# Order and distance of the loads in a linear attention step: alpha, then k and q, then v, and v two chunks ahead

## The chip, the cores and the metric

The kernel runs on one core of a Trainium2 chip. Its time is the device time of one execution in microseconds; of several executions the median is given. A profile is one further execution, recorded by the hardware profiler.

The engines are named as the profile names them: PE is TensorE (PEld its weight loads), DVE is VectorE, ACT is ScalarE, POOL is GpSimd, SP is SyncE, which in this kernel only issues DMA transfers (its queue is SPq). L144 is line 144 of the kernel.

## The reference

Two blocks follow each other. The first is a gated linear attention over 4 batches and 8 heads, 768 positions, head size 48, computed position by position:

```
state = alpha[t][:, None] * state + outer(k[t], v[t])
y[t]  = q[t] @ state
```

The second takes y as 3072 tokens of 384 features (8 heads times 48) and computes

```
a = x @ w1;  b = x @ w2          # 384 -> 1024 each
out = ((a * b) @ w3) @ w_out     # 1024 -> 1024 -> 384
```

Everything is float32 in the reference; the second block's weights arrive as 64-bit floats.

## The kernel before

**Attention in chunks.** The positions are cut into chunks of 128: six per batch, N = 24 in all, handled for all heads at once. For chunk n, `logs(n)` takes the logarithm of alpha on ACT (L271), `decays(n)` sums it along the positions with a triangular matrix on PE (L286 or L289) and takes exponentials on ACT (L292, L293), `decayed(n)` multiplies q and k by them on DVE (L302), `transposed(n)` transposes q and k on PE (L324) and copies them to `qkT` on ACT (L326), `scores(n)` multiplies them within the chunk on PE (L364), masked on DVE into `ms` (L367). `outer(n)` forms the sums of k and v that carry the state to the next chunk (PE L336, then DVE L344 or L346); the last chunk of a batch has none. The output comes from `attend_state(n)` (PE L384, the state's part) and `attend(n)` (PE L390, the chunk's own scores times v). Its copy on ACT (L394) is queued for a store to the DRAM buffer `xd`, written by SP at the next step's beginning (`store`, L261).

The chunk v(n) is thus read first by `outer(n)`, in step n of the main loop, and last by `attend(n)`, in step n + 1.

**Loads.** `load_a` (L132), `load_kq` (L138 for k, L139 for q) and `load_v` (L144) each issue transfers of 192 KB on SP's queue. alpha and the pair of k and q rotate through three buffers each. v has five fixed tiles, `vs`, made once with AHEAD = 4 in `AHEAD + 1`; v(n) lies in tile n modulo 5. Before the main loop the loads of the first chunks are issued with the setup and the first chunk's work between them. In step n of the main loop SP's part is, in the order of the source: the stores of the chunk before, a load of x back from `xd` in five of the steps (L406), then v(n + 3), alpha(n + 5), and k and q of n + 4.

**Weights.** The 64-bit weights w1 and w2 come in blocks of 512 KB (`raw`, L192, on the same SP queue), are turned into float32 on ACT and DVE and split into parts (`to_fp32`, `load_gates`, L200 to L221), with a third part formed on PE (`third`, L232 and L233) and copied by ACT (L234). `convert` and `fetch` deal this out in portions over the steps; four `raw` buffers exist.

**The gates and the rest.** From step 6 on x of three chunks is split into three parts (`split_x`, L412 on ACT, L413 and L414 on DVE), and the products with w1 and w2 (L420) are laid into the steps from 7 on as pieces of fill (`run`). After the main loop come the remaining gates, the product of w3 and w_out (`fold`, L522), and the last products with their output (`project`), again with L420 as the matmul's line.

**What sets the order.** The source gives each engine's instructions an order, and `after_marks` pins some of them behind named ones. Otherwise the order of each engine's queue is made when the kernel is built, by going through the program with estimates of when each input will be there; an instruction can stand behind others that follow it in the source. On the chip an engine runs its queue in that fixed order, and SP's queue in the profile is that of the source.[...]

Of the kernel before, what the change touches and what calls it, by code (L numbers as in the profile page):

```python
# [48 lines left out]
def kernel(  # L49
# [27 lines left out]
    AHEAD = 4  # L77
# [30 lines left out]
    def after_marks(*names):  # L108
        stack = ExitStack()
        for x in names:  # L110
            stack.enter_context(tc.issue_after(mark[x]))
        return stack
# [12 lines left out]
    def rows(src, n):  # L125
        b, c = divmod(n, NCH)
        return src[b, :, ds(c * C, C), :].rearrange("h p d -> p h d")

    def load_a(n):
        if n < N:  # L130
            st["a", n] = inp.tile([C, H, D], FP32, tag="ac", name="ac")
            nc.sync.dma_start(out=st["a", n], in_=rows(alpha, n))  # L132

    def load_kq(n):
        if n >= N:
            return
        st["kq", n] = inp.tile([C, 2, H, D], FP32, tag="kq", name="kq")
        nc.sync.dma_start(out=st["kq", n][:, 0], in_=rows(k, n))  # L138
        nc.sync.dma_start(out=st["kq", n][:, 1], in_=rows(q, n))  # L139

    def load_v(n):
        if n < N:
            st["v", n] = vs[n % len(vs)]
            nc.sync.dma_start(out=st["v", n][:, :, 0:D], in_=rows(v, n))  # L144
# [91 lines left out]
    def fetch(ahead=3):  # L236
        while weights and len(begun) < ahead:
            begun.append(weights.popleft())
            next(begun[-1])
# [17 lines left out]
    def store():  # L257

        while later:
            dst, src = later.popleft()  # L260
            nc.sync.dma_start(out=dst, in_=src)  # L261
# [4 lines left out]
    def logs(n):  # L266
        if n >= N:
            return
        a = st.pop(("a", n)).rearrange("p h d -> p (h d)")
        la = st["la", n] = work.tile([C, DM], FP32, tag="la", name="la")  # L270
        nc.scalar.activation(la, a, AF.Ln)  # L271
        if n >= LATE:

            t = st["la", n] = work.tile([C, 2, DM], FP32R, tag="la2", name="la2", bufs=1)
            nc.scalar.copy(t[:, 0], la)
            nc.vector.tensor_sub(t[:, 1], la, t[:, 0].bitcast(FP32))
        if n in ends:
            nc.gpsimd.dma_start(out=ends[n][2:3], in_=a[0:1])

    def decays(n):  # L280
        if n >= N:
            return
        lc = bank()[:, 0:DM]
        la = st.pop(("la", n))
        if n < LATE:
            nc.tensor.matmul(lc, sums[:, n % 2].bitcast(FP32), la, start=True, stop=True)  # L286
        else:
            for i in range(2):
                nc.tensor.matmul(lc, sums[:, n % 2], la[:, i], start=(i == 0), stop=(i == 1))  # L289

        e = st["e", n] = work.tile([C, 2, DM], FP32, tag="e", name="e", bufs=3)
        nc.scalar.activation(e[:, 0], lc, AF.Exp, scale=-1.0)  # L292
        mark["e", n] = nc.scalar.activation(e[:, 1], lc, AF.Exp).ins  # L293
        if n in ends:
            nc.gpsimd.dma_start(out=ends[n][0:1], in_=e[0:1, 0])
        if n + 1 in ends:
            nc.gpsimd.dma_start(out=ends[n + 1][1:2], in_=e[C - 1:C, 1])
        load_ends(n)

    def decayed(n):  # L300
        if n < N:
            mark["qk", n] = nc.vector.tensor_mul(qks[n % 3][:, :, :, 0:D], st.pop(("kq", n)),  # L302
                                 st.pop(("e", n)).rearrange("p i (h d) -> p i h d", h=H)).ins
# [9 lines left out]
    def transposed(n):  # L313
        if n >= N:
            return
        qk = qks[n % 3]
        qkT = work.tile([C, 2, NP, C], FP32, tag="qkT", name="qkT")

        tp = [bank().rearrange("p (i j c) -> p i j c", i=2, j=NP) for _ in range(2)]
        for i in range(2):  # L320
            for j in range(NP):
                for half in range(2):
                    s = ds(DP * half, DP)
                    nc.tensor.transpose(tp[half][:, i, j, :], qk[s, i, 2 * j:2 * j + 2, :], ident[s, s])  # L324
        for half in range(2):
            mark["qkT", n] = nc.scalar.copy(qkT[:, :, :, ds(DP * half, DP)], tp[half]).ins  # L326
        st["qkT", n] = qkT
# [30 lines left out]
    def scores(n):  # L358
        qkT = st["qkT", n]
        sc = [bank().rearrange("p (j c) -> p j c", j=NP) for _ in range(2)]  # L360
        for j in range(NP):
            for i in range(2):
                r = ds(DP * i, D)
                nc.tensor.matmul(sc[i][:, j, :], qkT[r, 0, j, :], qkT[r, 1, j, :], start=True, stop=True)  # L364
        ms = work.tile([C, 2, NP, C], FP32, tag="ms", name="ms")
        for i in range(2):
            masked = nc.vector.tensor_tensor(ms[:, i].bitcast(I32), sc[i].bitcast(I32), keep_bc, op=ALU.bitwise_and)  # L367
        ends_of_part1[0] = mark["ms", n] = masked.ins
        st["ms", n] = ms
# [3 lines left out]
    def attend_state(n):  # L373
        qkT = st.pop(("qkT", n))

        y = [bank()[:, 0:HP * C].rearrange("p (j c) -> p j c", c=C) for _ in range(2)]
        st["y", n] = y, [(half * HP + j, i, y[i][ds(DP * half, DP), j, :])
                         for j in range(HP) for i in range(2) for half in range(2)]  # L380
        if n % NCH:
            for j, i, to in st["y", n][1]:
                r = ds(DP * i, D)
                nc.tensor.matmul(to, Ts[n % 2][r, j, :], qkT[r, 1, j, :],  # L384
                                 start=(j % HP == 0), stop=False, skip_group_check=True)
# [18 lines left out]
    def load_x(g, queue=nc.sync):  # L404
        st["xT", g] = xp.tile([C, KM, TG], FP32, tag="xT", name="xT")
        queue.dma_start(out=st["xT", g], in_=xd[g].rearrange("(k p) t -> p k t", p=C))  # L406

    def split_x(g, i):
        x = st.pop(("xT", g))
        t = tr[i].tile([C, 3, KM, TG], FP32R, tag="x3", name="x3")  # L410
        st["x3", g] = t
        nc.scalar.activation(t[:, 0], x, AF.Copy, scale=1.0 - 2.0 ** -13)  # L412
        nc.vector.tensor_sub(t[:, 1], x, t[:, 0].bitcast(FP32))  # L413
        mark["x3"] = nc.vector.scalar_tensor_tensor(t[:, 2], t[:, 0].bitcast(FP32), -1.0 - 1.0 / P, x,  # L414
                                                    op0=ALU.mult, op1=ALU.add).ins
# [73 lines left out]
    def gate(g, f):  # L489
        yield from (late_gate if late else early_gate)(g, f)  # L490
# [97 lines left out]
    load_kq(2)  # L588
    load_a(3)
    decayed(1)  # L590
    load_v(2)
    load_kq(3)
    load_a(4)

# [4 lines left out]
    for n in range(N + 1):  # L599
        store()  # L600
        if n in loads:
            load_x(loads[n])
        load_v(n + AHEAD - 1)
        load_a(n + 5)
        load_kq(n + AHEAD)
        if n:
            attend_state(n - 1)
        if n < N:
            scores(n)
        transposed(n + 1)  # L610
        if n - 2 in begin:
            g, tiles = begin[n - 2]
            with after_marks(("ms", n), ("qkT", n + 1)):
                split_x(g, 0)
            fill.extend(gate(g, f) for f in tiles)
        pieces = (0, 3, 3, 2)[(n - 6) % 4] if n > 5 else 0
        if n == 0:
            with after_marks(("qkT", 0)):
                logs(2)
            decays(2)  # L620
            with after_marks(("e", 2)):
                logs(3)
        early, ready = n < 7, len(thirds)
        behind = after_marks(*[("qkT", n + 1)] * (n < N - 1), *[("qk", n + 1)] * early, *["x3"] * (n - 2 in begin))
        if n < N - 2:
            with behind:
                convert(2 if n == 0 else 1, 2 if n == 0 else 3 if n < 8 else 4)
        advance(n)
        if n:
            attend(n - 1)  # L630
        outer(n)
        third(ready)
        run(pieces > 0)
        if early:
            with after_marks(("qkT", n + 1), ("qk", n + 1)):
                convert(1)
        with after_marks(*[("ms", n)] * (n < 3)):
            decayed(n + 2)
        logs(n + 4)
        if n == 4:  # L640
            load_x(0)
        convert(early and n > 2)
        run(pieces > 1)
        decays(n + 3)
        if n < N - 2:
            convert(early or n % 3 == 0, 3 if n < 8 else 4)
        run(pieces > 2)
        if n == N - 3:
            while begun:
                convert(1)  # L650
            weights.extend(load_out(j) for j in range(KF))
            fetch(4)
# [91 lines left out]
```

## Time and profile before

| what | value |
|---|---|
| time, median of 3 executions (lowest, highest) | 480.89 us (480.33, 480.93) |
| the profiled execution: its own time | 478.61 us |
| its span in the profile | 476.8 us |
| PE busy in the span | 458.3 us |
| DVE, ACT busy | 356.3, 282.1 us |
| moved by DMA | 80.29 MB, mean 168 GB/s |
| loads of alpha, k, q, v | 24 each, 192 KB each |
| v, from issue to landing, median | 5.0 us |
| alpha, k, q, the same | 4.7, 5.4, 4.4 us |

The span runs from the first to the last recorded instruction; the execution's time is longer by what lies around it. Busy times overlap between the engines. The time from issue to landing of a transfer holds both its wait in the queue and the transfer itself.

### The profile page before, as it was taken

The numbers are of one execution on the slowest core, as the hardware profiler recorded it, in microseconds if no ns is written. First come the engines' busy times: TensorE is split into PE (matmuls) and PEld (weight loads), VectorE is DVE, ScalarE is ACT, GpSimd is POOL, SyncE is SP. The second block draws the span as 40 slices with busy tenths as digits, with TensorE's granted clock in tenths as the row PEclk, the third lists the DMA queues.
The fourth block names the chain that finished last, engine by engine and source line by source line (L and its number), as shares of the span: only waits on it lengthen the run. The fifth ranks groups of instructions, "written<-read, shape, count | busy, mean of one in ns | idle before, by whom it ended". The sixth has DMA issues, their size and how long they took to land.

```text
span 476.8 us, 10002 instructions
## 1 busy us (share of the span) xinstructions
PE 458.3 (96%) x3836; PEld 435.2 (91%) x3836; DVE 356.3 (75%) x576; ACT 282.1 (59%) x556; POOL 73.1 (15%) x140
## 2 busy tenths in 40 slices
PE   4879899999999999999999999999999999999996
PEld 2658589899899999999999999999999999999996
DVE  2769888886988988999998888745642876666761
ACT  4667766866758555898876666644545433333330
POOL 3321231112302310212331101202010100000000
PEclk9888889999999999999999999999999999999999
DMA  9999999999999964657775333122105965555511
GB/s 171 178 200 220 241 211 212 229 234 211 197 216 206 210 202 133 200 170 234 242 216 209 109 124 100 50 84 90 44 36 157 261 189 169 164 170 172 177 51 49
DMA packets 153583, 80.29 MB, mean 168 GB/s; under 512 B 104480, under 2 KB 145568, under 8 KB 153536
## 3 DMA queue, kind: packets, MB, share of 16 engines
q1 hardware_dynamic: 148016, 65.22, 56.8%
q0 software_dynamic: 5520, 14.43, 9.5%
q8 instruction: 30, 0.49, 0.5%
q14 instruction: 17, 0.14, 0.1%
HBM read 57.58 MB, written 22.06 MB: 167 GB/s over the span
## 4 chain that ended last, share of the span: by engine, by line
PE 87%; DMA 5%; SPq 3%; DVE 2%; ACT 1%; issue 1%; DVEq 0%; ACTq 0%
PE bank L420 70%; PE bank L364 5%; PE bank L390 4%; DMA raw<-in_moe_w_dram 4%; PE bank L384 2%; PE bank L324 2%; SPq L139 2%; PE bank L336 1%; PE bank L522 1%; PE bank L289 1%; DMA ac<-in_alpha_dram 1%; SPq L138 1%; SPq L132 1%; PE bank L286 1%; DVE ms L367 0%
## 5 line engine op out<-in xcount | busy, mean ns | idle before, releaser
L420 PE MATMUL bank<-x,w 128*128 128x384 f32 x1152 | 210.9, 337 | 0.0
L420 PEld LDWEIGHTS bank<-x,w 128*128 128x128 f32 x1152 | 200.4, 188 | 1.3 <-issue 0.7
L420 PE MATMUL bank<-w3o,ab 128*128 128x384 f32 x576 | 100.2, 336 | 0.0
L420 PEld LDWEIGHTS bank<-w3o,ab 128*128 128x128 f32 x576 | 99.9, 188 | 0.0
L445 ACT ACTIVATE bank<-bank 128x384 f32<-128x384 f32 x98 | 46.7, 477 | 43.6 <-PE bank L420 43.3
L429 ACT ACTIVATE t<-bank 128x384 f32<-128x384 f32 x62 | 30.6, 494 | 62.3 <-PE bank L420 60.1
L495 POOL DMA_DIRECT2D abd<-ab x46 | 26.9, 584 | 132.8 <-DVE ab L481 125.2
L481 DVE TENSOR_TENSOR ab<-bank,r 128x384 f32<-128x384 f32 x45 | 24.9, 552 | 23.4 <-ACT bank L445 18.6
L551 DVE TENSOR_TENSOR ab<-abl,ab 128x1024 fp32r<-128x1024 f32 x24 | 29.4, 1224 | 13.6 <-ACT ab L550 13.5
L550 ACT ACTIVATE ab<-abl 128x1024 fp32r<-128x1024 f32 x24 | 25.5, 1061 | 20.9 <-PE bank L420 19.2
L326 ACT COPY qkT<-bank 128x512 f32<-128x512 f32 x48 | 26.1, 591 | 19.0 <-PE bank L324 19.0
L367 DVE TENSOR_TENSOR ms<-bank,keep 128x512 int32<-128x512 int32 x48 | 31.4, 683 | 7.8 <-PE bank L364 7.8
L420 PE MATMUL bank<-wo,w3T 128*128 128x384 f32 x192 | 35.9, 334 | 0.0
L420 PEld LDWEIGHTS bank<-wo,w3T 128*128 128x128 f32 x192 | 33.5, 188 | 0.0
L364 PEld LDWEIGHTS bank<-qkT 48*128 48x128 f32 x384 | 25.7, 204 | 7.0 <-issue 4.2
L431 DVE SCALAR_TENSOR_TENSOR o<-bank,t 128x384 f32<-128x384 f32 x24 | 13.4, 557 | 24.0 <-issue 15.6
L364 PE MATMUL bank<-qkT 48*128 48x128 f32 x384 | 30.7, 304 | 0.4 <-ACT qkT L326 0.4
L552 DVE SCALAR_TENSOR_TENSOR ab<-ab,abl 128x1024 fp32r<-128x1024 f32 x24 | 29.2, 1217 | 0.0
L302 DVE TENSOR_TENSOR qk<-kq,e 128x768 f32<-128x768 f32 x24 | 23.0, 958 | 8.2 <-ACT e L293 8.1
L390 PE MATMUL bank<-ms,v 128*64 128x128 f32 x384 | 28.3, 293 | 0.0
L205 ACT ACTIVATE power<-power,rebias 128x512 uint32<-128x512 uint32 (+1 forms) x36 | 25.1, 701 | 4.1 <-DVE power L204 3.8
L200 ACT ACTIVATE rest<-raw 128x512 f32<-128x512 uint32 (+1 forms) x36 | 23.3, 650 | 7.1 <-DMA raw<-in_moe_w_dram 7.1
(80 smaller groups left out, 573.3 us busy)
## 6 DMA issues: line engine op xcount, KB each, us to landing
raw<-in_moe_w_dram SPq DMA_DIRECT2D x28, 512.0 KB, 5.2
abl<-abd SPq DMA_DIRECT2D x24, 512.0 KB, 4.6
abd<-ab POOLq DMA_DIRECT2D x46, 192.0 KB, 3.1
xT<-xd POOLq DMA_DIRECT2D x9, 576.0 KB, 4.5
ac<-in_alpha_dram SPq DMA_DIRECT2D x24, 192.0 KB, 4.7
kq<-in_k_dram SPq DMA_DIRECT2D x24, 192.0 KB, 5.4
kq<-in_q_dram SPq DMA_DIRECT2D x24, 192.0 KB, 4.4
v<-in_v_dram SPq DMA_DIRECT2D x24, 192.0 KB, 5.0
```

The source lines that it names most:

```text
L205: nc.scalar.activation(power, power, AF.Relu, scale=2.0 ** 23, bias=rebias)
L326: mark["qkT", n] = nc.scalar.copy(qkT[:, :, :, ds(DP * half, DP)], tp[half]).ins
L364: nc.tensor.matmul(sc[i][:, j, :], qkT[r, 0, j, :], qkT[r, 1, j, :], start=True, stop=True)
L367: masked = nc.vector.tensor_tensor(ms[:, i].bitcast(I32), sc[i].bitcast(I32), keep_bc, op=ALU.bitwise_and)
L390: nc.tensor.matmul(to, vc[:, 2 * j + i, :], ms[:, i, j, :], start=(n % NCH == 0 and j % HP == 0), stop=(j % HP == HP - 1), skip_group_chec ...
L420: nc.tensor.matmul(p, w[part][i], x[part][i], start=start and part == parts[0] and i == 0, stop=stop and part == parts[-1] and i == n - 1, ...
L429: nc.scalar.activation(t, p1, AF.Copy, scale=(1.0 + 1.0 / P) * scale)
L445: nc.scalar.activation(p, p, AF.Copy, scale=1.0 + 1.0 / P)
L495: (nc.gpsimd if late else nc.sync).dma_start(out=abd[g][:, f, :], in_=ab)
L550: nc.scalar.activation(t[:, 0], ab, AF.Copy, scale=1.0 - 2.0 ** -13)
L551: nc.vector.tensor_sub(t[:, 1], ab, t[:, 0].bitcast(FP32))
L552: nc.vector.scalar_tensor_tensor(t[:, 2], t[:, 0].bitcast(FP32), -1.0 - 1.0 / P, ab, op0=ALU.mult, op1=ALU.add)
```

## The change

The load of v moves behind those of alpha, k and q in each step, and fetches the chunk two ahead of the step's own in place of three. The load of v(2) ahead of the loop falls to step 0, which issues it in its new place. The five tiles of v stay. No other line changes.

```
--- before.py
+++ after.py
@@ -588,7 +588,6 @@
     load_kq(2)
     load_a(3)
     decayed(1)
-    load_v(2)
     load_kq(3)
     load_a(4)
 
@@ -600,9 +599,9 @@
         store()
         if n in loads:
             load_x(loads[n])
-        load_v(n + AHEAD - 1)
         load_a(n + 5)
         load_kq(n + AHEAD)
+        load_v(n + 2)
         if n:
             attend_state(n - 1)
         if n < N:
```

## The prediction

> **What bounds the kernel now.** I read the page's busy shares and slices first, then three wide stretches, then the chain that ended last, and last the SP and PE queues around 50 to 65 us. The page, busy times and slices of before:
>
> ```profile
> PE 458.3 (96%) x3836; PEld 435.2 (91%) x3836; DVE 356.3 (75%) x576; ACT 282.1 (59%) x556; POOL 73.1 (15%) x140
> ...
> PE   4879899999999999999999999999999999999996
> ...
> PEclk9888889999999999999999999999999999999999
> DMA  9999999999999964657775333122105965555511
> ```
>
> PE is full from the seventh slice on; DMA is full for the first fourteen. The same, as three stretches (busy us per engine, granted clock, DMA share, GB/s):
>
> ```profile
> 0.00:70.00 70.00, 55.61 (x634) 42.88 (x635) 47.78 (x85) 45.49 (x94) 18.18 (x47) 0.88 1.05 204
> 70.00:190.00 120.00, 119.58 (x1554) 109.84 (x1553) 102.44 (x178) 80.15 (x179) 21.50 (x39) 1.00 0.94 204
> 190.00:476.80 286.80, 283.07 (x1652) 282.48 (x1650) 206.05 (x315) 156.41 (x285) 33.44 (x54) 1.00 0.46 145
> ```
>
> After 70 us PE lacks 0.4 us up to 190 and 3.7 us to the end, nearly all of it the last output's tail (PE's last matmul ends near 473.1). So the end follows the moment from which PE is fed without a break. That moment is where the first gate matmuls (L420) begin, 64.27 us. In the first 70 us PE idles 14.4 us and runs part of the rest at half clock. What holds it there, from the chain:
>
> ```profile
> 30.59 0.88 SPq L139
> 31.52 6.32 DMA raw<-in_moe_w_dram
> ...
> 46.07 0.67 SPq L139
> 46.79 5.69 DMA raw<-in_moe_w_dram
> ```
>
> The chain runs through SP's issue of loads and the landing of weight blocks, again and again until 52.5 us. SP's queue in step n = 4:
>
> ```profile
> 49.04 0.46 SPq L144 DMA_DIRECT2D v<-in_v_dram  x1
> 49.55 0.92 SPq L132 DMA_DIRECT2D ac<-in_alpha_dram  x1
> 50.57 2.35 SPq L138 DMA_DIRECT2D kq<-in_k_dram  x1
> 52.96 0.86 SPq L139 DMA_DIRECT2D kq<-in_q_dram  x1
> 53.93 0.92 SPq L406 DMA_DIRECT2D xT<-xd  x1
> 54.89 0.49 SPq L192 DMA_DIRECT2D raw<-in_moe_w_dram  x1
> ```
>
> SP issues with hardly a pause and each issue takes as long as the queue lets it: the buffer of this k was freed by L302 at 40.7 us (39.73 and 0.95 long), ten microseconds earlier. Transfers set the pace here, not buffers. PE's queue at the same time (start, duration, idle time before and its releaser):
>
> ```profile
> 54.33 0.67 PE L336 MATMUL bank<-v,qk 128*64 128x48 f32 x16 [0.68 <-ACT x L394]
> ...
> 56.77 1.65 PE L286 MATMUL bank<-la,sums 128*128 128x384 f32 x2 [1.10 <-ACT la L271]
> 58.35 2.08 PE L364 MATMUL bank<-qkT 48*128 48x128 f32 x16
> ...
> 62.97 0.80 PE L336 MATMUL bank<-v,qk 128*64 128x48 f32 x16
> ...
> 64.27 3.31 PE L420 MATMUL bank<-x,w 128*128 128x384 f32 x18
> ```
>
> L336 is `outer`, the first reader of a v chunk: chunk 6 at 54.33, chunk 7 at 62.97. L286 waits for `logs(9)`, which waits for alpha 9.
>
> **What the Trainium skill says.** "DMA: Bandwidth & Descriptors", section "Queues, rings and completion order": on each DMA engine a queue's descriptors are consumed in ring order, so what SP issues first is served first. The trace agrees: landings of step 4 come at 54.0 (v), 55.4 (alpha), 56.2 (k) and 57.3 us (q). The same page, "Why small descriptors are slow (HBM only)", says that short packets carry a fixed overhead; v, alpha, k and q move in 192-byte runs (104480 of 153583 packets are under 512 B), and the first 70 us reach 204 GB/s. "TensorE: Matmul & The Clock Gate", section "Part 1: The HAM clock gate", says the clock is halved after an idle window of about 3.4 us and given back after a busy one, on windows that run freely. The trace agrees in kind: 0.50 granted from about 19.0 to 22.4, 32.8 to 39.5 and 56.5 to 63.3 us.
>
> **The change part by part.** No load is added or removed: 24 loads of v before and after, five v buffers still. Two things move.
>
> *v leaves the front of the stream.* Before, steps up to 0 issue v 0 to 3, and each later step one. After, v 3 waits for step 1, and so on: at every point of SP's queue after step 0's loads one v less has gone out. One such load is 196,608 B; at 204 GB/s that is 0.96 us. The landings of step 4 give (57.3 − 54.0)/3 = 1.1 us. I take 1.0. Weight blocks, x stores and the x load thus land 1.0 us earlier.
>
> *Inside a step v goes behind alpha, k and q.* SP is passed by one v more there, so alpha, k and q land two units, 2.0 us, earlier. Alpha 9: issued at 49.55, landed 5.8 later, 55.35; after, 53.4. v(n + 2) now lands where q(n + 4) landed, less one unit. From q's landings of before (issue plus its time to landing), with the start of `outer` on the right, itself taken 1.0 us earlier:
> - v 2: 27.2 − 1.0 = 26.2; 26.9. v 3: 35.5 − 1.0 = 34.5; 36.4. v 4: 42.9 − 1.0 = 41.9; 42.2. Just in time.
> - v 6: 57.3 − 1.0 = 56.3; 53.3. Late by 3.0.
> - v 7: 66.3 − 1.0 = 65.3; 62.0. Late by 3.3.
> - v 10: 87.4; 89.3. v 12: 101.5; 102.5. Later ones have about 1 to 4 us, but for v 15: 124.0; 122.3, late by 1.7 against a PE that is 1.0 us ahead.
>
> What an early wait would hold: behind `outer` on PE stand the weight thirds (L232, L233), `decays`, the next step's scores and the gates. Whether it holds them depends on where `outer` stands in PE's queue. The queues do not keep the source's order: `logs(9)` is traced in step 5, yet ran on ACT at 56.19, behind step 6's x copies (53.93), qkT copies (54.45) and L234 (55.71). It stands where alpha 9 was expected, and alpha 9 landed at 55.35. Where the order was made, landings were estimated close to the truth (in the first 35 us up to 2 us too early: ACT waited 1.97 for a block at 29.40). With v 6 three microseconds behind the readiness of `outer(6)`, I expect `outer` to be put behind the thirds, `decays(9)` and the scores. Nobody is in haste for it: its result is read by `attend_state(7)` a step later. Cost with that cover 0; without it, +2.3 (below).
>
> *The sum.* Step one, everything led by weight blocks and x: −1.0. Step two, the 1.10 us that PE waited for `logs(9)`: alpha lands 2.0 earlier, one unit of which is in step one, so between 0 and −1.1 more; L234 and L271 share ACT, so I take half, −0.5. Step three, late v: 0, ends 0 and +3.3 (a load that comes later can't itself gain). Step four, clock: a half-clock window more or less is 3.4 us at half speed, ±1.7; I take 0, as the same gaps remain. Removing the wait of v's buffer on SP is 0: it was for `attend` of five chunks before, done long ago. Sum −1.5: 478.61 us of the profiled execution become 477.1. The median of before, 480.89, lies 2.28 above that execution (span 476.8 and 1.8 around it); so 479.4 for the median.
>
> How much could come at best: gates need x 0, loaded at 53.93 and landed 5.3 later, 59.2; 58.2 after; its split on ACT takes 1.16 and on DVE 1.35: 60.8, so −3.5 and 477.4. The second half of the stretch gives nothing more, as PE is full.
>
> **The rivals.**
> - *The late v takes the place of the wait removed (slower).* If `outer(6)` and `outer(7)` keep their places, PE stands until v 6 at 56.3, against a start at 54.33 (+2.0), and until v 7 at 65.3 against 62.97 (+2.3; it contains the first). After that PE is full and cannot make it up: 483.2. It decides once `outer` stands in PE's queue over 1 us ahead of v's landing. For it: L336 stood right behind L390 in every early step, and early estimates were too early. Against it: `logs` was moved back in just this way.
> - *Nothing reaches the end (same).* DVE is 9.2 to 9.8 us busy of each 10 us between 30 and 50 us and PE's start at 64.27 also needs ACT and DVE for the split; a small stall of a late v eats the unit gained. 480.4 to 481.4. Against it: DVE's stretch itself begins with a weight block (waited for 2.11 us at 29.40).
> - *The whole room is used (faster).* Alpha, k and q two units ahead pull `decays` and the scores forward, the gates start at 60.8 and the 1.01 us wait of L289 at 68.59 shrinks: 477.4 or a little less.
>
> **How the numbers follow.** Likeliest, order adjusts and the end moves 0.5 to 3 us: 0.50, own range 477.9 to 480.4, at 479.4. Late v: 0.21. Nothing: 0.17. Whole room: 0.12. What a measurement can tell from no change is 0.2%, 0.96 us, so faster means under 479.9. Of the likeliest 0.44 is faster and 0.06 same. Faster 0.44 + 0.12 = 0.56; same 0.06 + 0.17 = 0.23; slower 0.21. Range: 477.0 leaves out half of a larger gain than worked out, 483.0 about half of the late v and its cold windows.
>
> **What would show it.** Right: weight blocks from the second on land about 1 us earlier (the one at 52.5 near 51.5), alpha 9 near 53.4; L336 of chunk 6 runs behind L286 or L364; the first L420 starts at 61 to 63.5 us; PE still lacks nothing from 70 us. Wrong: L336 with an idle time before it released by v's DMA, two to three us at 53 and 62 us; or the first L420 at 64 us or later; or half clock over the gates after 64 us.

## The result, and the profile after

The changed kernel is slower: 481.74 us (median of 21 executions, 479.24 to 484.82) against 480.19 us for the kernel before on the same chip (21 executions, 477.11 to 482.27). The ratio is 1.0037, 95% interval 1.0021 to 1.0053. Measured again it is 1.0028 (1.0014 to 1.0042; 480.63 against 479.06 us). The forecast was a gain of 1.5 us (479.4 from 480.89). The measured loss of 1.3 to 1.8 us has the sign, and somewhat over half the size, of what the rival "the late v takes the place of the wait removed" gave, +2.3.

The page of the profile after, busy times and slices (tenths of each of 40 equal slices):

```profile
PE 458.1 (95%) x3836; PEld 434.2 (91%) x3836; DVE 356.8 (74%) x576; ACT 280.0 (58%) x556; POOL 73.5 (15%) x140
...
PE   4889789899899999999999999999999999999996
...
PEclk9999899899999999999999999999999999999999
DMA  9999999989999954557675443122104965555511
```

PE's work is the same 458 us; only its place in time differs. The profiled execution took 481.45 us, its span is 479.7. The same three stretches (busy us per engine, granted clock, DMA share, GB/s):

```profile
0.00:70.00 70.00, 55.30 (x653) 42.31 (x653) 49.96 (x89) 48.06 (x100) 19.77 (x48) 0.95 1.03 210
70.00:190.00 120.00, 116.82 (x1524) 106.57 (x1517) 98.53 (x169) 73.15 (x166) 20.35 (x39) 1.00 0.88 199
190.00:479.70 289.70, 285.95 (x1669) 285.36 (x1667) 208.34 (x319) 158.84 (x292) 33.35 (x54) 1.00 0.46 144
```

In the first 70 us PE idles 14.7 us at a clock of 0.95, where before it idled 14.4 at 0.88: with more of the full clock it still does no better. From 70 to 190 us it now lacks 3.2 us, where it lacked 0.4. So in these two profiles two places differ. The first is in PE's queue (start, duration, idle time before and its releaser):

```profile
50.44 1.09 PE L390 MATMUL bank<-ms,v 128*64 128x128 f32 x16
54.45 1.10 PE L336 MATMUL bank<-v,qk 128*64 128x48 f32 x16 [2.91 <-DMA v<-in_v_dram]
...
56.50 1.35 PE L286 MATMUL bank<-la,sums 128*128 128x384 f32 x2
...
62.72 0.67 PE L336 MATMUL bank<-v,qk 128*64 128x48 f32 x16 [1.98 <-DMA v<-in_v_dram]
...
63.89 3.38 PE L420 MATMUL bank<-x,w 128*128 128x384 f32 x18
```

`outer(6)` and `outer(7)` (L336) stand right behind `attend` (L390), where they stood before, and each waits for its v. The thirds, `decays(9)` (L286), the scores and then the gates (L420) stand behind them. L286 has no wait of its own any more: alpha 9 was there. The loads are in SP's queue and in the chain that ended last:

```profile
45.50 0.47 SPq L132 DMA_DIRECT2D ac<-in_alpha_dram  x1
...
46.94 2.46 SPq L139 DMA_DIRECT2D kq<-in_q_dram  x1
49.50 0.66 SPq L144 DMA_DIRECT2D v<-in_v_dram  x1
```

```profile
49.50 4.81 DMA v<-in_v_dram
...
54.45 1.10 PE bank L336 x16
...
58.63 3.95 DMA v<-in_v_dram
...
62.72 0.67 PE bank L336 x16
```

v 6 lands at 54.3 us and v 7 at 62.6, and PE starts each `outer` within 0.15 us of that. The landing of v is now a link of the chain that ended last, where in the profile of before it was none. The second place is later, and landings of alpha are links of the same chain there (issued at 83.84, 115.01 and 122.38 us, 4.6 to 6.4 us each), so that the chain names two suspects and prices neither. ACT's logarithms (L271) wait for alpha 22.0 us in all, ten times, where they waited 6.0 us five times before. One of the long ones, in ACT's queue:

```profile
90.29 0.52 ACT L271 ACTIVATE la<-ac 128x384 f32<-128x384 f32 x1 [3.07 <-DMA ac<-in_alpha_dram]
```

### The profile page after: what moved, and what is told of

It reads as the page before. It is cut to its first block, busy times and chain, and to the rows that moved or that the text cites. A ratio compares the mean times of both kernels' runs of the same rounds, so it can differ in the third digit from the quotient of the medians.

```text
span 479.7 us, 9992 instructions
## 1 busy us (share of the span) xinstructions
PE 458.1 (95%) x3836; PEld 434.2 (91%) x3836; DVE 356.8 (74%) x576; ACT 280.0 (58%) x556; POOL 73.5 (15%) x140
## 4 chain that ended last, share of the span: by engine, by line
PE 87%; DMA 7%; ACT 2%; SPq 2%; DVE 1%; issue 1%; DVEq 0%; ACTq 0%
PE bank L420 69%; DMA ac<-in_alpha_dram 4%; PE bank L364 4%; PE bank L390 4%; PE bank L324 2%; DMA v<-in_v_dram 2%; PE bank L384 2%; PE bank L286 2%; PE bank L336 2%; PE bank L522 1%; DMA raw<-in_moe_w_dram 1%; PE bank L289 1%; SPq L261 1%; PE bank L232 1%; ACT qkT L326 0%
## 5 line engine op out<-in xcount | busy, mean ns | idle before, releaser
L420 PE MATMUL bank<-x,w 128*128 128x384 f32 x1152 | 210.9, 337 | 0.9 <-ACT qkT L326 0.9
L420 PEld LDWEIGHTS bank<-x,w 128*128 128x128 f32 x1152 | 200.2, 188 | 2.6 <-ACT qkT L326 1.2
L420 PE MATMUL bank<-w3o,ab 128*128 128x384 f32 x576 | 100.2, 336 | 0.0
L420 PEld LDWEIGHTS bank<-w3o,ab 128*128 128x128 f32 x576 | 99.9, 188 | 0.0
L420 PE MATMUL bank<-wo,w3T 128*128 128x384 f32 x192 | 35.9, 334 | 0.0
L420 PEld LDWEIGHTS bank<-wo,w3T 128*128 128x128 f32 x192 | 33.5, 188 | 0.0
L364 PEld LDWEIGHTS bank<-qkT 48*128 48x128 f32 x384 | 24.9, 199 | 7.9 <-issue 3.1
L364 PE MATMUL bank<-qkT 48*128 48x128 f32 x384 | 29.7, 297 | 0.8 <-ACT qkT L326 0.8
L390 PE MATMUL bank<-ms,v 128*64 128x128 f32 x384 | 27.8, 289 | 0.1
L207 DVE SCALAR_TENSOR_TENSOR mant<-mant,rest 128x512 f32<-128x512 uint32 (+1 forms) x36 | 24.2, 673 | 3.5 <-ACT rest L200 3.4
```

The lines of the kernel that those rows point to most:

```text
L390: nc.tensor.matmul(to, vc[:, 2 * j + i, :], ms[:, i, j, :], start=(n % NCH == 0 and j % HP == 0), stop=(j % HP == HP - 1), skip_group_chec ...
L420: nc.tensor.matmul(p, w[part][i], x[part][i], start=start and part == parts[0] and i == 0, stop=stop and part == parts[-1] and i == n - 1, ...
```

## The experiments

Three theories were open. (1) The late v costs the time, and the new order inside the step is a gain that it outweighs. (2) The logarithms that wait for alpha cost it: the build put `logs` further ahead in ACT's queue (`logs(13)` behind 10 pairs of qkT copies instead of 11, `logs(14)` behind 11 instead of 13), and in the DMA-bound stretch alpha is not there. (3) The clock costs it: PE's gaps end in half-speed windows. Ratios are against the kernel before, measured on the same chip in turn.

**The two parts apart.** One kernel keeps v three ahead and moves it behind alpha, k and q; the other fetches v two ahead and leaves it in front.

```
-        load_v(n + AHEAD - 1)
         load_a(n + 5)
         load_kq(n + AHEAD)
+        load_v(n + AHEAD - 1)      # order alone (load_v(2) ahead of the loop kept)
```

> Order part alone: alpha, k and q, then v of the chunk three ahead, v(2) ahead of the loop as before. First theory (alpha's logarithms stand too early in ACT's queue, so that ACT and then PE wait for alpha after 80 us): the logarithms stand here where they stood before, so no alpha waits on ACT of over 1 us after 64 us, PE idle from 70 to 190 us under 1 us, and the time 1 us below before to equal (0.997 to 1.001). Second theory (late v at outer of chunks 6 and 7): v is in time, the same forecast. It splits both from a third, that the order of the loads costs by itself on SP (then 1.003).

```
-        load_v(n + AHEAD - 1)
+        load_v(n + 2)              # distance alone (no load_v(2) ahead of the loop)
         load_a(n + 5)
         load_kq(n + AHEAD)
```

> Distance part alone: v first in its step, but of the chunk two ahead. First theory: alpha lands one unit earlier and the logarithms of chunks 14, 18, 21 and 22 stand a copy earlier on ACT than before; alpha waits of 1 to 2 us there, PE idle from 70 to 190 us 0.5 to 2 us, time 0.998 to 1.003. Second theory: v of chunk 6 lands near 53 us, no wait at outer, time 0.996 to 1.000.

Order alone: 0.9976 (0.9963 to 0.9988), 1.1 us faster. Distance alone: 1.0005 (0.9984 to 1.0026), no difference that can be told. So the two parts do not add up to the whole: −1.1 and about 0 apart, +1.3 to +1.8 together. In the second, v 6 is in time but v 7 is still late by 3.71 us, although it is issued first in its step, so two chunks of distance are too few even there. PE's queue with order alone:

```profile
53.91 0.67 PE L336 MATMUL bank<-v,qk 128*64 128x48 f32 x16
...
59.75 0.62 PE L336 MATMUL bank<-v,qk 128*64 128x48 f32 x16
...
61.17 0.79 PE L420 MATMUL bank<-x,w 128*128 128x384 f32 x3
```

No wait for v, and the gates begin 2.72 us earlier than with the whole change (63.89). By the ratios the whole change is 2.5 to 2.9 us slower than order alone. That the two figures are alike proves little: in the other four profiles of the changed kernel, further below, the gates begin at 64.85 to 65.86 us.

**The late v mended, the rest of the change kept.** v 6 and v 7 go out one step earlier, in steps 3 and 4; all other loads stand as in the changed kernel. A second version moves v 7 alone, into step 4; the two differ in the line of the `for`.

```
-        load_v(n + 2)
+        for m in {3: (5, 6), 4: (7,), 5: ()}.get(n, (n + 2,)):    # v 6, 7 early
+            load_v(m)
```

```
-        load_v(n + 2)
+        for m in {4: (6, 7), 5: ()}.get(n, (n + 2,)):             # v 7 early
+            load_v(m)
```

> The changed kernel with the loads of v of chunks 6 and 7 alone issued one step earlier each. Late v with its half clock (the theory now first): no wait of outer for v near 54 and 63 us, clock back to 0.990 or more, time 0.996 to 1.000 of before. Alpha's place on ACT as the main cause: two loads change little, time 1.001 to 1.004.

> The changed kernel with the load of v of chunk 7 alone issued one step earlier; that of chunk 6 stays late. If the last wait before the gates sets the price: 0.997 to 1.000 of before, as with both early (0.9973). If both waits add up: 0.999 to 1.002, half way to the changed kernel's 1.003.

v 6 and 7 early: 0.9973 (0.9958 to 0.9988; 477.92 against 479.06 us), with the changed kernel at 1.0028 beside it. Two loads of v moved by one step are worth 2.6 us. Neither `outer` waits for v any more. PE's queue:

```profile
52.97 0.67 PE L336 MATMUL bank<-v,qk 128*64 128x48 f32 x16
...
58.81 0.62 PE L336 MATMUL bank<-v,qk 128*64 128x48 f32 x16
...
60.24 0.79 PE L420 MATMUL bank<-x,w 128*128 128x384 f32 x3 [0.16 <-ACT x L412]
```

The loads are not all that differs, though. With v earlier, the build also put `logs(13)` and `logs(14)` back behind 11 and 12 pairs of qkT copies, and ACT waits 7.2 us for alpha in place of 22.0. This pair alone thus does not part theory (1) from theory (2); the pinned pair below does.

v 7 alone early: 0.9987 (0.9968 to 1.0005); `outer(6)` still waits 3.26 us, `outer(7)` does not, the gates begin at 61.68. The time lies between, as does the wait.

Not every earlier place will do. With v put ahead of alpha in steps 4 and 5 alone:

```
+        if n in (4, 5):
+            load_v(n + 2)
         load_a(n + 5)
         load_kq(n + AHEAD)
-        load_v(n + 2)
+        if n not in (4, 5):
+            load_v(n + 2)
```

> The changed kernel with v first in steps 4 and 5 alone, so that v of chunks 6 and 7 land some 3 us earlier. First theory: the waits at outer (2.9 and 2.0 us) go and the first gate matmul starts 1 to 2 us earlier, but alpha waits on ACT after 80 us grow by as much, and the time stays at 1.001 to 1.004 of before. Second theory: the time falls to 0.994 to 0.999 of before.

1.0003 (0.9979 to 1.0026). v 6 is in time (0.25 us of wait, for another input), but PE stands 3.45 us ahead of `outer(7)`, which starts at 61.93, right after v 7's landing (issued at 55.37, 6.4 us to land), and the gates begin at 63.97. First in its own step is too late for v 7, as in distance alone. Set against v 6 and 7 early (0.9973), the three kernels give a price for each wait: `outer(6)` alone late costs 0.7 us (0.9987), `outer(7)` alone 1.4 (1.0003), both 2.6 (1.0028). The intervals leave each of these uncertain by about 1 us, so it is in keeping with two waits that add, and no more than that.

**The reverse: the late v put into the good kernel.** In order alone, v 6 and 7 are held back by one step.

```
-        load_v(n + AHEAD - 1)
+        for m in {3: (), 4: (6,), 5: (7, 8)}.get(n, (n + AHEAD - 1,)):
+            load_v(m)
```

> The order part alone, which ran at 0.9976, with the loads of v of chunks 6 and 7 alone issued one step later each. Late v with its half clock: outer waits 2 to 4 us in all for v, the clock falls to 0.984 to 0.988 and the time rises by 2 to 4 us to 1.001 to 1.006. If v is not the cause: 0.996 to 0.999.

1.0095 (1.0072 to 1.0117; 483.77 us), by the ratios 5.7 us slower than order alone, and slower than the 1.001 to 1.006 that was expected. PE's queue:

```profile
56.20 0.85 PE L336 MATMUL bank<-v,qk 128*64 128x48 f32 x16 [2.98 <-DMA v<-in_v_dram]
...
65.19 0.67 PE L336 MATMUL bank<-v,qk 128*64 128x48 f32 x16 [2.82 <-ACT power L205]
```

The two idle times are 5.8 us together. (The second is put down to ACT, whose own work on the weight blocks runs at the same moment; nothing that L336 reads comes from it.) The late v thus brings a loss wherever it is set, and taking it away brings the gain. The size is not understood: in the changed kernel the loads of v 6 and v 7 stand in the same steps, behind the same alpha, k and q; its two waits are together 4.9 to 5.4 us long in its five profiles, and on the same chip it took 480.63 us, 3.1 less than this one.

**The place in PE's queue.** The forecast had put `outer(6)` and `outer(7)` behind the work that follows. This kernel does that by hand, with the loads of the changed kernel untouched:

```
-        outer(n)
+        if n not in (6, 7):
+            outer(n)
...
         run(pieces > 2)
+        if n in (6, 7):
+            outer(n)
```

> The changed kernel, loads and all, with outer of chunk 6 placed behind the decays of its step on PE and outer of chunk 7 behind the first gate's matmuls, which is where the prediction expected them. If their place in PE's queue is what the prediction had wrong: no wait for v over 0.5 us, first gate matmul at 60 to 62 us, time 0.995 to 0.999 of before. If late v costs by another way (DVE, ACT): 1.001 to 1.004.

0.9995 (0.9979 to 1.0011): 1.6 to 2.0 us better than the changed kernel's two measurements. PE's queue:

```profile
55.62 0.67 PE L336 MATMUL bank<-v,qk 128*64 128x48 f32 x16 [0.89 <-DMA v<-in_v_dram]
...
59.39 1.42 PE L420 MATMUL bank<-x,w 128*128 128x384 f32 x6
...
65.54 0.67 PE L336 MATMUL bank<-v,qk 128*64 128x48 f32 x16
```

`outer(6)` now has the thirds and `decays` ahead of it and still waits 0.89 us, over the 0.5 expected; `outer(7)` runs after the first gates, without a wait. v 6 and v 7 are issued at 50.00 and 58.72 us, as late as in the changed kernel (49.50 and 58.63); it is the place in the queue that made them cost. Here too the build put `logs` back (ACT waits 7.7 us for alpha), but that alone brings no gain, as the next kernels show. The span is 475.8 us, as with v early (475.9).

**The logarithms that wait for alpha.** The loads of the changed kernel stay as they are. First `logs` is pinned, from step 7 on, behind the qkT copies of its step, and then the work on the weight blocks of DVE and ACT is pinned too (behind the masked scores, `ms`).

```
-        logs(n + 4)
+        with after_marks(*[("qkT", n + 1)] * (n > 6 and n < N - 1)):
+            logs(n + 4)
```

> The changed kernel with each logarithm of alpha from chunk 11 on held, on ACT, behind the qkT copies of the chunk three before. First theory: the qkT copies no longer wait behind alpha; PE idle from 70 to 190 us falls from 3.2 to under 1 us and the time falls by 2.5 to 4 us against the changed kernel, to 0.994 to 0.999 of before. Second theory: the late v is untouched, so the time stays at 1.002 to 1.005 of before.

```
-        behind = after_marks(*[("qkT", n + 1)] * (n < N - 1), ..., *["x3"] * (n - 2 in begin))
+        behind = after_marks(*[("qkT", n + 1)] * (n < N - 1), ..., *[("ms", n)] * (6 < n < N), *["x3"] * (n - 2 in begin))
+            if n > 7 and n % 3 == 1:           # ahead of the step's first convert
+                with after_marks(("ms", n)):
+                    convert(1, 4)
...
-        if n < N - 2:                          # the step's last convert
+        if n < N - 2 and (n < 7 or n == N - 3):
```

> The changed kernel with alpha's logarithms held behind qkT on ACT as in the earlier run and, from step 8 on, the weight conversions on DVE held behind the masks of their step. If the order of ACT's and DVE's queues after step 8 costs what the changed kernel lost there: no stop of PE near 90 us, the stretch from outer of chunk 8 to the end 403 to 404.5 us in place of about 405.4, time 0.998 to 1.001 of before. If the late v alone is the price: 1.002 to 1.004.

The first takes ACT's wait for alpha from 22.0 to 6.6 us: 1.0031 (1.0013 to 1.0049). The second takes it to 4.0 us, and PE lacks nothing at all between 70 and 190 us (120.00 busy of 120.00): 1.0026 (1.0012 to 1.0040). Both lie within the intervals of the unpinned kernel (1.0037 and 1.0028). So the waits that stand out most in ACT's list have no price that these timings can tell, and theory (2) falls as the main cause. In the second kernel v 7 was again what PE waited for:

```profile
63.69 1.10 PE L336 MATMUL bank<-v,qk 128*64 128x48 f32 x16 [4.17 <-DMA v<-in_v_dram]
...
65.74 3.79 PE L420 MATMUL bank<-x,w 128*128 128x384 f32 x18
```

Add the early v 6 and 7 to this pinned kernel, and it turns fast:

> The same, and the loads of v of chunks 6 and 7 one step earlier. If both costs are real and add up: 0.993 to 0.996 of before, under the 0.9973 of the early loads alone. If a kernel that is ahead at step 8 gives it back for want of its inputs: 0.996 to 0.999.

0.9985 (0.9973 to 0.9998; 476.91 against 477.95 us), 2.0 us better than the pinned kernel with the late v, measured on the same chip. `logs(13)` and `logs(14)` stand behind 11 and 12 pairs of copies in both, so this pair shows the price of the late v apart from theory (2). `outer` runs at 52.91 and 58.74 us, the gates begin at 60.16. It is not faster than the unpinned kernel with v early (0.9973); PE idles 2.46 us between 100 and 130 us here.

**The clock.** The changed kernel has a lower mean granted clock (0.986 over its executions, order alone 0.991, v early 0.992). To part the clock from the wait, matmuls that nobody reads fill PE's gaps ahead of `outer(6)` and `outer(7)` in the changed kernel: 8 and 5 of them, then 10 and 15. They stand behind `attend`'s last matmul, to which `attend` is made to leave a mark (not shown), and `outer` behind them.

```
-        outer(n)
+        if n in (6, 7):
+            p = bank()
+            with after_marks("attend"):
+                for _ in range((8, 5)[n - 6]):          # (10, 15) in the second
+                    mark["warm"] = nc.tensor.matmul(p, signs[:, 0], w12[0][:, 0, 0, 0, :], start=True, stop=True).ins
+            with after_marks("warm"):
+                outer(n)
+        else:
+            outer(n)
```

> The changed kernel with 8 matmuls of 128x512 ahead of outer of chunk 6 and 5 ahead of that of chunk 7, their result unused, in the time in which PE waits for v (about 2.7 and 1.7 us at full clock). If the half clock after those waits is a large part of the price: clock back to 0.990 or more, time 2 us or more under the changed kernel, 0.997 to 1.000 of before. If the price is the waiting itself: no change or slower, 1.003 to 1.006.

> The changed kernel with 10 unused matmuls of 128x512 ahead of outer of chunk 6 and 15 ahead of that of chunk 7 (2.7 and 4.0 us at full clock), since 5 left 2.9 us of waiting before chunk 7. Half clock as the larger part of the price: granted clock 0.991 or more, also from 64 to 70 us, time 0.998 to 1.001 of before. Place of the start of the gates as the price: clock up, time still 1.002 to 1.004.

1.0031 (1.0015 to 1.0047) and 1.0037 (1.0022 to 1.0052), at mean clocks of 0.989 and 0.992. In the second, the matmuls of line 634 fill the gap and the clock is full throughout 50 to 70 us, and yet:

```profile
59.45 3.76 PE L634 MATMUL bank<-w,signs 128*128 128x512 f32 x15 [0.18 <-ACT qkT L326]
64.10 0.67 PE L336 MATMUL bank<-v,qk 128*64 128x48 f32 x16 [0.89 <-DMA v<-in_v_dram]
...
65.28 3.31 PE L420 MATMUL bank<-x,w 128*128 128x384 f32 x18
```

PE still waits for v 7 after all its idle matmuls, and the gates begin when v 7 lets them. The clock is given back and the time is not: theory (3) falls as the main cause. That v 7 landed 1.4 us later in this trace than in the first of the changed kernel keeps a small share of the clock from being excluded.

**How far one profile can be trusted.** The kernel before once more, and the changed kernel four times more, one of these with repeated timing:

> The kernel before, another profile: no wait of outer for v, outer of chunk 8 between 71 and 74 us, PE idle from 70 to 130 us under 1.5 us.

> The changed kernel once more, beside the next three on one chip: 1.002 to 1.005 of before, mean granted clock near 0.986, by every theory.

> The changed kernel, another profile. Late v in every execution: outer of chunks 6 and 7 wait 4 to 6 us in all for v, outer of chunk 8 starts at 72.5 to 75 us. Alpha's place on ACT in some executions alone: PE idle from 70 to 130 us anywhere between 0.4 and 3.2 us.

> The same once more: v waits of 4 to 6 us again, the idle time of PE from 70 to 130 us larger where outer of chunk 8 starts earlier.

> The same once more: v waits of 4 to 6 us again, the idle time of PE from 70 to 130 us larger where outer of chunk 8 starts earlier.

PE's queue of the kernel before, second profile:

```profile
60.29 0.62 PE L336 MATMUL bank<-v,qk 128*64 128x48 f32 x16
...
61.41 1.55 PE L420 MATMUL bank<-x,w 128*128 128x384 f32 x6
```

The gates of before begin at 61.41 us here and at 64.27 in the profile that the prediction read. The difference is the clock: it was granted at 0.58 from 60 to 64 us in that profile, and at 1.00 in this one, and the matmuls just ahead took that much longer (the scores, L364, 2.08 against 1.16 us; `attend`, L390, 1.97 against 1.09). The two executions still differ little in time (478.61 and 479.41 us), for the second has later waits (57.40 us of PE's work between 70 and 130, against 59.58; under 1.5 us of idle time had been expected). In the five profiles of the changed kernel the gates begin at 63.89 to 65.86 us, each time behind an `outer(7)` that had waited.

The second place, between 70 and 190 us, does not stand up to this comparison at all. PE lacks 3.2 us there in the first profile of the changed kernel and 0.5, 2.0, 1.2 and 1.3 in the other four; of the kernel before it lacks 0.4 in one profile and 2.6 in the other. The 3.2 against 0.4 with which the search began lies within what executions of one kernel differ by.

## Why the prediction was wrong

**The step that failed** is step three of the sum, "late v: 0", with its ground: "With v 6 three microseconds behind the readiness of `outer(6)`, I expect `outer` to be put behind the thirds, `decays(9)` and the scores." It was not moved by one place: PE stood 2.9 and 2.0 us before it, and the step priced at 0 cost 2.0 to 2.9 us. That `logs(9)` had been traced out of the source's order was read as proof that the build would move `outer` too; it was proof only that the build can move an instruction. Why it left `outer` is not shown; the prediction had itself noted that the estimates of landings can come out too early, which may be the reason. With `outer` moved by hand the loss is gone (0.9995), so it was the place that failed. But the gain of 1.5 us (0.997) does not come with it: the interval, 0.9979 to 1.0011, leaves it out.

**The size of the rival was about right for this kernel.** "Cost with that cover 0; without it, +2.3": three comparisons put it at 2.6 us (v early against the changed kernel), 2.0 (the same with the pins) and 2.5 to 2.9 (order alone against the changed kernel); the fourth, the late v set into order alone, gave 5.7. In the changed kernel it is set against the gain below, so the balance is +1.3 to +1.8 and not +2.3. The point "over 1 us ahead of v's landing" held: the two waits are 2.9 and 2.0 us.

**The landings were late by about the right amount, at other times.** v 6 was to land at 56.3 us and landed at 54.3, v 7 at 65.3 and 62.6, alpha 9 at 53.4 and 50.5, the weight block of 52.5 at 51.5 and 48.9. All came 2 to 3 us earlier than worked out. PE came to the two `outer` earlier too, but by less (at 51.5 for 53.3, and at 60.7 for 62.0), so that v 6 was late by 2.9 us as worked out (3.0), and v 7 by 2.0 and not 3.3. One load of v less ahead was priced at 1.0 us; the same block went out to SP's queue at 43.82 us here and at 46.59 with order alone, 2.8 earlier. Between two kernels that had by then issued the same loads (order alone and v early) that issue differs by 1.1 us as well, so 2.8 is not all due to the load; why the stream ran so far ahead stays open.

**Steps one and two, −1.0 and −0.5.** A gain of the forecast size is there: order alone −1.1 us, v 6 and 7 early −1.3 (0.9973 of 479.06). But it was put to the wrong part. The prediction drew two thirds of it from one v less in the stream; order alone, which has no v less and only issues alpha, k and q one load earlier, brings it already. The wait for `logs(9)` ahead of L286 falls from 1.10 to 0.33 us there. What the shorter stream is worth by itself no run shows cleanly: distance alone, which has it, gained nothing (1.0005) but had a late v 7; v early adds it for part of the steps and is not told apart from order alone.

**"PE still lacks nothing from 70 us"** was wrong, and did not hold for every execution of the kernel before either (2.6 us lacking in the second). The prediction took any lead at 64 us to last to the end. The traces show PE held by other inputs once it is ahead (57.4 to 58.2 us of PE's work between 70 and 130 in order alone, v early and the second profile of before), so part of a lead is given back. With v early the gates begin 4.6 us before those of the changed kernel on the same chip (60.24 and 64.85), and the medians lie 2.7 us apart; in the pinned pair it is 5.6 us (60.16 and 65.74) and 2.1. The 60.8 us that the prediction gave as the best start was passed by three kernels (59.39 to 60.24), and none came near the −3.5 us that it was to bring. That the logarithms of ACT were put ahead of the qkT copies was not foreseen either; ACT waited for alpha because of it, but pinning it back changed the time by no more than the intervals.

**Step four, clock 0 ± 1.7,** was fair as a range, but the start it was set against, 64.27 us, held a half-clock window that another execution did not have. Counted from 61.41 us the change of the start is +2.5 to +4.5 over the five profiles, not −0.4.

The signs named for "wrong" were the ones to see: L336 with two to three us of idle time released by v's DMA near 53 and 62 us, and the first L420 near 64 (63.89, and 64.85 or later in the other profiles).

## What to carry to other kernels

When a load is moved back, set its new landing against its first reader's place in the engine's queue as it is, and price the whole queue behind that reader; count on a reordering only where that same instruction has been seen to give way. Where a change has two parts, measure them apart and together: the order alone gained 1.1 us, the distance alone neither gained nor lost, and the distance on top of the order lost 2.5 or more; issuing two of the loads one step earlier kept the gain (0.9973). A wait that is long in the list of waits may be no price at all: ask what else would hold the end at the same place. And before a stretch is explained by the change, see in a second profile of each kernel whether it differs at all.

## What was unexpected of the hardware

The half-speed windows of TensorE do not follow from the kernel alone. The Trainium skill, "TensorE: Matmul & The Clock Gate", section "Part 1: The HAM clock gate (the "warmup" mystery)", says that an idle window of about 3.4 us throttles the array. The trace does not agree to the letter: in the 3.4 us ahead of the slow stretch (53.1 to 56.5 us) PE was busy for 1.90 us, and no gap was longer than 1.10 us. The second profile of the same kernel has gaps much like these (0.21 and 1.10 us in place of 0.68 and 1.10, 2.21 us busy in the same 3.4) and kept the full clock: 0.58 over 60 to 64 us in one, 1.00 in the other, and gates that began 2.9 us apart for it. And the end hardly followed: 0.8 us between the two executions, in the other direction. Restoring the clock with unread matmuls (0.986 to 0.992 mean) did not bring the changed kernel's ratio down (1.0037 and 1.0028 without them, 1.0037 with them).
